# Eight of 36 split gate/up pieces: stored in pass one, or split again late in pass two; the third piece in the buffer of the sums

## The chip, the cores and the metric

The kernel runs on one core of a Trainium2 chip. The metric is the device time of one execution in microseconds (us), measured on the chip; lower is better. TensorE (PE in the profile), VectorE (DVE), ScalarE (ACT), GpSimd (POOL) and SyncE (SP, which here only issues transfers) run side by side, each through its own list of instructions in order. Transfers between HBM and the on-chip memory run on 16 DMA engines.

## The reference

x has 2048 rows of 576 numbers. It is normalized by rows (xn), and two branches take xn: an attention with 32 heads of 18 columns, and a bilinear gated unit with 4608 columns. The result is x + attention * silu(gated unit).

```python
qkv = xn @ wqkv                        # 32 heads of 18
p = softmax(q @ k.T * 18 ** -0.5)      # 2048 x 2048 for each head
s = concat(p @ v) @ wo
g = xn @ w_gate                        # 576 x 4608
u = xn @ w_up
b = (g * u) @ w_down                   # 4608 x 576
out = x + s * silu(b)
```

All is float32.

## The kernel before

**Numbers in two parts.** Products take float32r operands. Each operand is split into a rounded part (an ACT copy) and the rest (a POOL subtraction), and a product is three matmuls: high by high, rest by high, high by rest.

**Stages.** A prologue normalizes x, makes q, k and v and stores them to HBM. The main stage runs attention and the gated unit together in one list of PE instructions. The last stage multiplies by wo, forms silu of the last rows and writes out.

**The gated unit.** The 2048 rows are taken in NCH = 4 passes of 512 (c = 0 to 3). In each pass the 4608 columns are taken in NF2 = 18 units of 256, so there are 72 units; a unit u has two pieces, n = 2u and n = 2u + 1, 144 in all, and a piece is 128 columns of w_up and w_gate together. The columns go up in passes one and three and down in two and four (`columns_of`, L158), so the unit at a turn keeps its weights. PE's array is used as two halves of 64 rows with a stream of matmuls each (`stream`, L848): stream 0 multiplies the up columns of a piece, stream 1 its gate columns, 27 matmuls each (L678); `up_end` (L681) evicts on ACT (L683), `gate_end` (L685) multiplies on DVE (L690), then splits the product into hs on ACT (L693) and POOL (L694). The down product of unit u - 1 follows the two pieces of unit u in each stream (L720): it needs hs and hx, which is hs with the two halves of its rows exchanged by two transfers (`turn_round`, L700 to L710). Its results are added into `acc` by DVE (L746, L748).

**Gate and up weights.** In pass one, piece n is loaded raw (`g_raw`, L113: two transfers of 288 KB into one of the two `wraw` buffers), split by `g_get` (L169) as three "chores" of an ACT copy (L193) and a POOL subtraction (L194) each, and a fourth chore, `end` (L197), stores the split piece to HBM (`swg`, 1152 KB, L199) and loads the raw piece n + 2. In passes two to four `g_get` loads the split piece from `swg` (L185). Split pieces live in two `wgu` buffers; `gate_end` of piece n calls `g_get(n + 2)` (L691), since piece n's buffer is free then. The down weights have a like scheme with one buffer (`d_get`, L208; `draw`, `swd`, `wd`); `draw` is later used by silu of finished rows (`silu_store`, L781).

**Attention.** For each of 32 heads there are 64 "a" matmuls (L596), whose 128 x 512 results DVE reduces to row maxima (L598); then `max_rows` (L606) puts the maxima into the operands; then 64 "b" matmuls (L628), on which ACT takes the exponential (L630); then groups of up to seven key tiles are multiplied by v (L639), over the whole array.

**The order.** `order` (L1111) writes PE's list. It keeps a clock for each stream and guesses of when engines and transfers are done, and picks what comes next. Attention items have due times on this clock (`a_goal`, L929; `b_goal`, L932); the gated unit fills in. A stream may not begin piece n before `loaded[n - 2]` (L1082), which is set when gate piece n - 2 ends (L1178), with a guess of a 1.18 MB transfer for every piece, in pass one too. `there["h", u]` (L1182, L1171) is the guessed arrival of hx. `small` (L1003) hands out one chore at a time, when ACT is thought to be free. Matmuls wait on the chip only where the real event is later than the place in the list.

All transfers named above are issued by SP in the order in which the program emits them; each issue waits there for what it depends on.

Of the kernel before, what the change touches and what calls it, by code (L numbers as in the profile page):

```python
# [40 lines left out]
def kernel(  # L41
# [70 lines left out]

    def g_raw(f):  # L113
        raw = wpool.tile([128, 9, 128], FT, name="wraw", bufs=2)
        for r, m in enumerate((w_up, w_gate)):
            nc.sync.dma_start(raw[64 * r:64 * r + 64], m[:, 128 * f:128 * f + 128].rearrange("(b p) c -> p b c", p=64))
        return raw
# [45 lines left out]
    gdone, ddone = set(), set()  # L163

    def g_load(n):
        if n < 2 * NF2:
            graw[n] = g_raw(n)

    def g_get(n):  # L169
# [9 lines left out]
        if n > 1 and n // 2 % NF2 == 0:  # L179
            gw[n] = gw[n - 2]  # L180
            gdone.add(n)
            return
        w = gw[n] = g_tile()
        if n >= 2 * NF2:
            nc.sync.dma_start(w.bitcast(FT), swg[f])  # L185
            gdone.add(n)
            return
# [9 lines left out]
        def end():  # L197
            gdone.add(n)
            nc.sync.dma_start(swg[f], w.bitcast(FT))  # L199
            g_load(n + 2)  # L200

# [376 lines left out]
    with ExitStack() as mid:  # L578
# [106 lines left out]
        def gate_end(n, ps):  # L685
# [4 lines left out]
            nc.vector.tensor_tensor(h32, ps, h32, op=OP.mult)  # L690
            g_get(n + 2)  # L691
            hj = hs[u][:, j]
            nc.scalar.activation(hj[:, 0, :], h32, AF.Copy)  # L693
            nc.gpsimd.tensor_tensor(hj[:, 1, :], h32, hj[:, 0, :].bitcast(FT), op=OP.subtract)  # L694
            if u == 0 and j or u == len(units) - 1:
                turn_round(u, j)
# [3 lines left out]
        def turn_round(u, j):  # L700
# [5 lines left out]
            else:  # L706
                hx[u] = gp.tile([128, 2, 2, 512], FR, name="hx", bufs=1)
                js = slice(0, 2)
            for r in range(2):
# [401 lines left out]
        def order():  # L1111
            nonlocal na, nb
            load_v(0)
            feeds = [stream(0), stream(1)]
            heads.extend(next(f) for f in feeds)
            wait = None
            while any(heads) or na < TOTAL or nb < TOTAL or due:
# [35 lines left out]
                elif op is not None:  # L1153
# [8 lines left out]
                    if end:  # L1162
# [11 lines left out]
                        else:  # L1174
                            gated[n] = done
                            fin = engine("ACT", done + 0.05, 0.535)
                            fin = engine("POOL", fin + 0.05, 1.29)
                            loaded[n] = moved(done - 0.4, 1.18) if (n // 2 + 1) % NF2 else 0.0  # L1178
                            if n // 2 == len(units) - 1:
                                there["h", n // 2] = moved(fin, 0.524)  # L1180
                            elif n == 1:
                                there["h", 0] = moved(fin, 1.05)  # L1182
                            for _ in range(2):
# [10 lines left out]

        heads, stuck, parts, loaded, stacks = [], [False], {}, {}, []
        order()


# [115 lines left out]
```

## Time and profile before

| what | us |
|---|---|
| median of three runs | 2569.61 |
| lowest and highest of them | 2569.59, 2571.27 |
| the profiled execution, its own time | 2571.43 |
| its span in the profile | 2569.4 |
| prologue (up to the first main matmul) | 0 to 195 |
| main stage | 195 to 2501 |
| last stage | 2501 to 2569 |

The span is the time between the first and the last recorded instruction. Busy times of an engine are sums over its instructions. A busy PE says that at least one matmul was under way, not that both halves of its array had one; how many matmuls ran in a stretch (the number behind x) tells that.

### The profile page before, as it was taken

The numbers are of one execution on the slowest core, as the hardware profiler recorded it, in microseconds if no ns is written. First come the engines' busy times: TensorE is split into PE (matmuls) and PEld (weight loads), VectorE is DVE, ScalarE is ACT, GpSimd is POOL, SyncE is SP. The second block draws the span as 40 slices with busy tenths as digits, with TensorE's granted clock in tenths as the row PEclk, the third lists the DMA queues.
The fourth block names the chain that finished last, engine by engine and source line by source line (L and its number), as shares of the span: only waits on it lengthen the run. The fifth ranks groups of instructions, "written<-read, shape, count | busy, mean of one in ns | idle before, by whom it ended". The sixth has DMA issues, their size and how long they took to land.

```text
span 2569.4 us, 59203 instructions
## 1 busy us (share of the span) xinstructions
PE 2547.8 (99%) x24360; PEld 2111.1 (82%) x24360; DVE 1933.2 (75%) x3377; ACT 1467.1 (57%) x2688; POOL 594.8 (23%) x663
## 2 busy tenths in 40 slices
PE   8999999999999999999999999999999999999999
PEld 7899888878878888877888888777888877888878
DVE  6208778777778898777778888777888887778437
ACT  5222666666756665555665665555665655556651
POOL 3214434434421111111111111111111111111125
PEclk9999999999999999999999999999999999999999
DMA  7799988888886666665686656665686666654567
GB/s 243 235 284 278 263 226 225 232 225 220 221 206 186 176 182 177 175 179 155 179 197 173 179 175 184 176 170 154 179 204 166 180 184 176 175 174 146 159 189 248
DMA packets 195898, 504.58 MB, mean 196 GB/s; under 512 B 58112, under 2 KB 116352, under 8 KB 156588
## 3 DMA queue, kind: packets, MB, share of 16 engines
q1 hardware_dynamic: 185676, 489.05, 68.6%
q0 software_dynamic: 9952, 11.74, 1.7%
q8 instruction: 192, 3.15, 0.6%
q14 instruction: 78, 0.64, 0.1%
HBM read 312.21 MB, written 107.61 MB: 163 GB/s over the span
## 4 chain that ended last, share of the span: by engine, by line
PE 95%; DMA 3%; DVE 1%; SPq 0%; ACT 0%; issue 0%; POOL 0%; ACTq 0%; DVEq 0%
PE pg L678 34%; PE pg L639 18%; PE pg L720 16%; PE pa L596 12%; PE pb L628 8%; PE pg L402 2%; PE pa L348 2%; PE pb L348 2%; PE pg L1244 1%; DMA hx<-hs 1%; PE pb L1244 1%; PE pa L1244 1%; DMA sqk<-hl 0%; DMA ring<-sqk 0%; DMA xc<-sx 0%; DMA o<-sot 0%
## 5 line engine op out<-in xcount | busy, mean ns | idle before, releaser
L598 DVE TENSOR_REDUCE mx<-pa 128x1 f32<-128x512 f32 x2048 | 1367.1, 686 | 223.6 <-PE pa L596 104.8
L630 ACT ACTIVATE pt<-pb 128x512 f32<-128x512 f32 x2048 | 1161.9, 598 | 534.8 <-PE pb L628 465.5
L678 PE MATMUL pg<-xc,wgu 64*128 64x512 f32 x7776 | 1366.1, 388 | 0.7 <-DMA xc<-sx 0.5
L678 PEld LDWEIGHTS pg<-xc,wgu 64*128 64x128 f32 x7776 | 1051.7, 184 | 41.6 <-DMA xc<-sx 1.2
L628 PE MATMUL pb<-pair,ring 64*128 64x512 f32 x1997 | 777.4, 395 | 1.5 <-DMA ring<-sqk 1.5
L596 PE MATMUL pa<-pair,ring 64*128 64x512 f32 x2006 | 776.9, 393 | 1.8 <-DVE mx L598 1.8
L720 PE MATMUL pg<-wd,hs 64*128 64x288 f32 x3408 | 523.4, 292 | 0.0
L720 PE MATMUL pg<-wd,hx 64*128 64x288 f32 x3408 | 515.2, 292 | 2.4 <-DMA hx<-hs 2.4
L694 POOL TENSOR_TENSOR hs<-us,hs 128x512 fp32r<-128x512 f32 x144 | 186.2, 1293 | 1320.3 <-ACT hs L693 1285.6
L720 PEld LDWEIGHTS pg<-wd,hs 64*128 64x128 f32 x3408 | 459.8, 185 | 4.0 <-DVE acc L748 0.2
L720 PEld LDWEIGHTS pg<-wd,hx 64*128 64x128 f32 x3408 | 453.4, 185 | 6.5 <-DMA hx<-hs 3.0
L639 PE MATMUL pg<-pt,vt 128*32 128x512 f32 x4096 | 454.8, 594 | 0.7 <-DVE acc L748 0.6
L596 PEld LDWEIGHTS pa<-pair,ring 64*128 64x128 f32 x2006 | 364.3, 184 | 69.8 <-issue 52.8
L628 PEld LDWEIGHTS pb<-pair,ring 64*128 64x128 f32 x1997 | 362.5, 184 | 8.7 <-issue 1.9
L639 PEld LDWEIGHTS pg<-pt,vt 128*32 128x32 f32 x4096 | 125.5, 110 | 284.0 <-issue 278.9
L748 DVE TENSOR_TENSOR acc<-acc,pg 128x288 f32<-128x288 f32 x544 | 233.0, 443 | 22.4 <-PE pg L720 21.4
L645 DVE TENSOR_TENSOR oc<-oc,pg 128x512 f32<-128x512 f32 x69 | 47.1, 683 | 220.4 <-PE pg L639 213.7
L693 ACT ACTIVATE hs<-us 128x512 fp32r<-128x512 f32 x144 | 91.0, 632 | 151.0 <-DVE us L690 149.7
L194 POOL TENSOR_TENSOR wgu<-wraw,wgu 128x384 fp32r<-128x384 f32 x108 | 108.6, 1017 | 97.1 <-ACT wgu L193 84.6
L643 ACT ACTIVATE oc<-pg 128x512 f32<-128x512 f32 x32 | 19.2, 598 | 185.0 <-PE pg L639 179.0
L690 DVE TENSOR_TENSOR us<-pg,us 128x512 f32<-128x512 f32 x144 | 98.2, 682 | 26.9 <-PE pg L678 15.7
L618 POOL DMA_DIRECT2D pair<-mt x128 | 77.8, 613 | 166.4 <-DVE mt L613 162.3
(141 smaller groups left out, 1359.0 us busy)
## 6 DMA issues: line engine op xcount, KB each, us to landing
wgu<-swg SPq DMA_DIRECT2D x102, 1152.0 KB
hx<-hs SPq DMA_DIRECT2D x142, 512.0 KB
wd<-swd SPq DMA_DIRECT2D x50, 1152.0 KB
swg<-wgu SPq DMA_DIRECT2D x36, 1152.0 KB
pair<-sqk SPq DMA_DIRECT2D x192, 144.0 KB
ring<-sqk SPq DMA_DIRECT2D x384, 72.0 KB
swd<-wd SPq DMA_DIRECT2D x18, 1152.0 KB
sqk<-hl SPq DMA_DIRECT2D x32, 512.0 KB
```

The source lines that it names most:

```text
L194: nc.gpsimd.tensor_tensor(w[:, 9 + b:12 + b, :], raw[:, b:b + 3, :], w[:, b:b + 3, :].bitcast(FT), op=OP.subtract)
L348: nc.tensor.matmul(p, wq[b, a], xcs[c][:, e, :], start=n == 0, stop=n == len(PAIRS) - 1)
L596: nc.tensor.matmul(p, q[rows, t * 128:(t + 1) * 128], k[rows, c * 512:(c + 1) * 512], start=True, stop=True)
L598: nc.vector.tensor_reduce(mx[h][:, t, c:c + 1], p, axis=AX.X, op=OP.max)
L628: nc.tensor.matmul(p, k[rows, t * 128:(t + 1) * 128], q[rows, c * 512:(c + 1) * 512], start=True, stop=True)
L630: nc.scalar.activation(pt[t, c], p, AF.Exp, scale=scale)
L639: nc.tensor.matmul(p[32 * c:32 * c + 32, :], vt[h // 2][:, t, 6 * (h % 2):6 * (h % 2) + 32], pt[t, c], start=t == ts[0], stop=t == ts[-1])
L678: nc.tensor.matmul(ps, gw[n][half[r], a, :], xg[i][half[r], e, :], start=k == 0, stop=k == len(TERMS) - 1)
L690: nc.vector.tensor_tensor(h32, ps, h32, op=OP.mult)
L694: nc.gpsimd.tensor_tensor(hj[:, 1, :], h32, hj[:, 0, :].bitcast(FT), op=OP.subtract)
L720: nc.tensor.matmul(ps[:, 0:HALF], (hx if k else hs)[u][half[r], j, a, s * 128:(s + 1) * 128], dw[u][half[r], k, j, e, :], start=n == 0, st ...
L748: nc.vector.tensor_tensor(a, a, ps[:, 0:HALF], op=OP.add)
```

## The change

The split pieces with f < 8 (columns 0 to 1023, pieces n = 0 to 7 of pass one) are not stored in pass one. In pass two these columns come last, as n = 64 to 71; there they are loaded raw into the `draw` buffer (one buffer), split again by chores and stored to `swg` then, for passes three and four. The raw load of n = 64 is issued with `g_get(62)`, each further one by the chore `end` of the piece ahead of it.

Piece n = 2 gets a buffer of its own, the one that later holds the sums (`acc`), and is asked for at the start of `order`. So `gate_end` of pieces 0 and 1 asks for pieces 3 and 4, that of piece 2 for none, and from 3 on it is n + 2 as before. The hx transfers of unit 0 are issued in halves, after each of its two pieces. The guesses in `order` follow.

```diff
-    def g_raw(f):
-        raw = wpool.tile([128, 9, 128], FT, name="wraw", bufs=2)
+    def g_raw(f, tag, bufs):
+        raw = wpool.tile([128, 9, 128], FT, name="wraw", tag=tag, bufs=bufs)
...
+    UNSAVED = 8
+
+    def g_after(n):
+        return {0: 3, 1: 4, 2: None}.get(n, n + 2)
+
     def g_load(n):
         if n < 2 * NF2:
-            graw[n] = g_raw(n)
+            graw[n] = g_raw(n, "wraw", 2)
+        elif 4 * NF2 - UNSAVED <= n < 4 * NF2:
+            graw[n] = g_raw(2 * columns_of(n // 2) + n % 2, "draw", 1)
...
-        w = gw[n] = g_tile()
-        if n >= 2 * NF2:
+        w = gw[n] = accp.tile([128, 18, 128], FR, name="wg2", tag="acc") if n == 2 else g_tile()
+        anew = 2 * NF2 <= n < 4 * NF2 and f < UNSAVED
+        if n == 4 * NF2 - UNSAVED - 2:
+            g_load(n + 2)
+        if n >= 2 * NF2 and not anew:
             nc.sync.dma_start(w.bitcast(FT), swg[f])
...
             gdone.add(n)
-            nc.sync.dma_start(swg[f], w.bitcast(FT))
-            g_load(n + 2)
+            if f >= UNSAVED or anew:
+                nc.sync.dma_start(swg[f], w.bitcast(FT))
+            g_load(n + 1 if anew else n + 2)
...
-            g_get(n + 2)
+            if g_after(n):
+                g_get(g_after(n))
...
-            if u == 0 and j or u == len(units) - 1:
+            if u in (0, len(units) - 1):
                 turn_round(u, j)
...
-                hx[u] = gp.tile([128, 2, 2, 512], FR, name="hx", bufs=1)
-                js = slice(0, 2)
+                if u or j == 0:
+                    hx[u] = gp.tile([128, 2, 2, 512], FR, name="hx", bufs=1)
+                js = slice(0, 2) if u else slice(j, j + 1)
...
             load_v(0)
+            g_get(2)
...
-                            loaded[n] = moved(done - 0.4, 1.18) if (n // 2 + 1) % NF2 else 0.0
+                            if n != 2:
+                                loaded[g_after(n) - 2] = moved(done - 0.4, 1.18) if (n // 2 + 1) % NF2 else 0.0
...
-                            elif n == 1:
-                                there["h", 0] = moved(fin, 1.05)
+                            elif n < 2:
+                                there["h", 0] = moved(fin, 0.524)
...
-        heads, stuck, parts, loaded, stacks = [], [False], {}, {}, []
+        heads, stuck, parts, loaded, stacks = [], [False], {}, {0: 0.0}, []
```

## Rows read from the trace of the kernel before

**Rows 1.** The page: busy time of the engines, and the DMA share in 40 slices.

```profile
PE 2547.8 (99%) x24360; PEld 2111.1 (82%) x24360; DVE 1933.2 (75%) x3377; ACT 1467.1 (57%) x2688; POOL 594.8 (23%) x663
DMA  7799988888886666665686656665686666654567
```

**Rows 2.** Windows: stretch, length, busy (x count) of PE, PEld, DVE, ACT, POOL, clock, DMA share, GB/s.

```profile
200.00:205.00 5.00, 5.00 (x47) 4.96 (x45) 4.34 (x7) 0.60 (x1) 0.00 (x0) 1.00 1.00 336
210.00:215.00 5.00, 5.00 (x32) 3.76 (x32) 4.60 (x8) 1.40 (x3) 1.36 (x2) 1.00 1.30 213
275.00:280.00 5.00, 3.56 (x42) 3.32 (x44) 2.60 (x5) 2.24 (x5) 1.30 (x1) 1.00 0.85 249
280.00:285.00 5.00, 5.00 (x70) 4.96 (x68) 4.89 (x11) 3.71 (x8) 3.06 (x3) 1.00 0.82 228
```

**Rows 3.** Timeline of ACT: evictions of up pieces 1 and 2 (start, duration).

```profile
208.80 0.60 ACT L683 ACTIVATE us<-pg 128x512 f32<-128x512 f32 x1 [1.18 <-PE pg L678]
218.72 0.60 ACT L683 ACTIVATE us<-pg 128x512 f32<-128x512 f32 x1 [3.20 <-PE pg L678]
```

**Rows 4.** Timeline of POOL: the split of piece 2.

```profile
207.72 2.96 POOL L194 TENSOR_TENSOR wgu<-wraw,wgu 128x384 fp32r<-128x384 f32 x3
```

**Rows 5.** Timeline of PE: a down matmul of unit 2; in brackets the idle time before.

```profile
276.24 0.40 PE L720 MATMUL pg<-wd,hx 64*128 64x288 f32 x1 [2.23 <-DMA hx<-hs]
```

**Rows 6.** Timeline of SP: transfers issued ahead of hx of unit 2 (start, issue time).

```profile
253.64 0.33 SPq L199 DMA_DIRECT2D swg<-wgu  x1
...
260.85 0.34 SPq L199 DMA_DIRECT2D swg<-wgu  x1
...
264.19 3.28 SPq L710 DMA_DIRECT2D hx<-hs  x2
```

**Rows 7.** Chain of waits: the same hx, start and length.

```profile
266.87 11.50 DMA hx<-hs
```

**Rows 8.** Windows of longer stretches (columns as in rows 2).

```profile
195.00:335.00 140.00, 136.80 (x1314) 121.18 (x1316) 110.78 (x188) 64.40 (x122) 63.18 (x60) 1.00 1.03 270
...
735.00:775.00 40.00, 37.98 (x387) 30.51 (x385) 29.66 (x56) 24.13 (x43) 8.00 (x9) 1.00 0.75 187
1200.00:1320.00 120.00, 120.00 (x1186) 97.98 (x1184) 94.13 (x166) 70.97 (x128) 18.05 (x23) 1.00 0.69 181
```

**Rows 9.** The page: the stores of split pieces (count, KB each).

```profile
swg<-wgu SPq DMA_DIRECT2D x36, 1152.0 KB
```

**Rows 10.** Timeline of DVE: ends of gate pieces, in pass one and late in pass two.

```profile
390.22 0.68 DVE L690 TENSOR_TENSOR us<-pg,us 128x512 f32<-128x512 f32 x1
...
1208.21 0.68 DVE L690 TENSOR_TENSOR us<-pg,us 128x512 f32<-128x512 f32 x1
1223.65 0.68 DVE L690 TENSOR_TENSOR us<-pg,us 128x512 f32<-128x512 f32 x1
```

**Rows 11.** Timeline of SP: the store of the piece asked for at 390.22.

```profile
401.92 0.34 SPq L199 DMA_DIRECT2D swg<-wgu  x1
```

**Rows 12.** Windows: a stretch in which the transfers of pass two run.

```profile
1207.00:1214.00 7.00, 7.00 (x65) 6.55 (x65) 6.34 (x10) 4.78 (x9) 1.29 (x1) 1.00 0.96 268
```

**Rows 13.** Groups of instructions: the split's ACT step (busy, mean ns, idle before).

```profile
L193 ACT ACTIVATE wgu<-wraw 128x384 fp32r<-128x384 f32 x108 | 54.1, 520 | 2.0 <-DMA wraw<-in_B_w_gate_dram 2.0
```

**Rows 14.** Timelines at the first head's maxima: DVE, POOL, and PE's wait after it.

```profile
247.64 0.78 DVE L610 TENSOR_SCALAR mm<-m 128x16 fp32r<-128x16 f32 x1
...
247.36 2.00 POOL L194 TENSOR_TENSOR wgu<-wraw,wgu 128x384 fp32r<-128x384 f32 x2
...
250.26 0.50 PE L596 MATMUL pa<-pair,ring 64*128 64x512 f32 x1 [0.77 <-DVE mx L598]
```

**Rows 15.** One line of the kernel: L610, all 32 (duration min/median/max in ns).

```profile
L610 DVE TENSOR_SCALAR mm<-m x32: 174/174/1187, 247.6 to 2405.9; 128x16 fp32r<-128x16 f32 x32
```

**Rows 16.** Chain of waits near the end of the main stage.

```profile
2481.92 3.57 PE pg L639 x32
...
2487.67 5.00 PE pg L720 x68
```

## The prediction

> **What bounds the kernel now.** The page comes first: PE is busy 99% of the span, so no other engine is the bound, and DMA is nearly full only in the slices from the second to the tenth [rows 1]. But a busy PE can have half its array empty, so the next view is the count of matmuls. At 200 to 205 us, while only piece and "a" matmuls run, 47 of them fit in 5 us, 5.00 / 47 = 0.106 us each; at 210 to 215 the same kinds reach only 32, with PE still "busy 5.00" [rows 2]. At 275 to 280, with down matmuls, 42 run where the next 5 us hold 70 [rows 2]. Then the wide stretches: from 195 to 335 PE idles 140.00 - 136.80 = 3.20 us and DMA is at a share of 1.03; late in pass two (1200 to 1320) PE idles nowhere and DMA is at 0.69 [rows 8]. I read from this that time can be won nearly only in the first 140 us of the main stage, by two things.
>
> The first is the hold of stream 0. Up piece 1 is evicted at 208.80, up piece 2 only 9.92 us later, at 218.72 [rows 3]. Piece 2 was split by POOL from 207.72 to 210.68 [rows 4], since its buffer was free only when gate piece 0 had ended; and the order holds the stream by its guess of a 1.18 MB transfer from that end. PE doesn't idle there, it runs one stream.
>
> The second is hx of unit 2. SP issues it at 264.19, behind two stores of split pieces (253.64, 260.85) [rows 6]; in the chain its transfer takes 11.50 us from 266.87 [rows 7], and PE stands for 2.23 us until the first part is there [rows 5].
>
> **The change, part by part.**
>
> *Piece 2 in its own buffer.* Its raw weights are loaded before the main stage starts. The three ACT copies and three POOL subtractions move from 207.7 to about 195, where ACT and POOL have nothing to do (0.60 and 0.00 us busy at 200 to 205 [rows 2]), so the move itself costs nothing; without that cover it would cost POOL's 2.96 us [rows 4]. Stream 0 goes on with up piece 2 at about 209. Pieces 3 and 4 are then asked for when gate pieces 0 and 1 end, one piece earlier than they are needed, which is the old lead again. The gain is the empty half: 47 - 32 = 15 matmuls at 0.106 us = **1.6 us** [rows 2]. Bounds: 0 if another guess (hx, the next piece) holds the stream instead, 2.1 us if the stream held were full otherwise: 27 matmuls at 2 x 0.106 are 5.7 us, the evictions lie 9.92 apart [rows 3], and half of the 4.2 us between is 2.1. The halved hx of unit 0 is two more issues on SP; hx is needed some 10 us after, so I take 0 for it.
>
> *Eight stores fewer in pass one.* Two stores of 1152 KB go from ahead of hx of unit 2 [rows 6, 9], 2.36 MB, at 270 GB/s [rows 8] 8.7 us of the transfer queue. Then hx, complete at 266.87 + 11.50 = 278.37 [rows 7], would be complete near 269.6, ahead of PE's need at 276.24 - 2.23 = 274.0 [rows 5]. PE's wait goes whole: **2.2 us**. What is late next: unit 0's and unit 1's hx have no wait on PE now, and have fewer stores ahead too; the stores begin again with piece 8, behind hx of unit 2. The lower end is 0 (hx held by something else than the queue), the upper end all that PE idles from 195 to 335, 3.20 us [rows 8].
>
> *Eight pieces anew in pass two.* Removed: eight loads of 1.18 MB; added: eight raw loads (two issues each) of half that and eight stores of 1.18 MB, so 8 x 0.59 = 4.7 MB more in some 125 us. DMA stands at 0.69 there [rows 8], and 4.7 MB at 268 GB/s [rows 12] is 18 us, 0.14 more: still room. SP gets 8 issues more, and the store waits on SP for POOL where the load waited for PE; behind it stand hx and the attention's loads, as in pass one, where from 335 on PE loses nothing that I see. ACT gets 24 x 0.520 = 12.5 us [rows 13] on 70.97 of 120 busy [rows 8], POOL 24 us (three in 2.96 [rows 4]) on 18.05: neither becomes the bound.
>
> The new wait is that of the ACT copy for its raw piece: one `draw` buffer, so the raw load of the next piece is issued only after the split of this one. In pass one the store that follows a split came 401.92 - 390.22 = 11.7 us after the gate end that asked for it [rows 10, 11]; store and raw load are 1.77 MB, at 268 GB/s [rows 12] 6.6 us. So raw is there 18.3 us after that gate end. The next gate end comes 1223.65 - 1208.21 = 15.44 us after the first [rows 10], and its chores start at once or some us later. So ACT stands 0 to 2.9 us for each of seven pieces, the exponentials queued behind it, and PE waits for these through the two pb banks. A second bank lets PE go on for about one spacing of the exponentials (2048 of them, 32 x 64, over some 2300 us of main stage: 1.1 us), so PE loses 0 to 1.8 us a piece, 0 to 12.6 us in all. I take **0.5 us lost**, near the lower end, since chores are handed out only when ACT is thought to be free and the 11.7 us held a visit to the v product.
>
> *A collision of POOL and DVE.* At 247.64 the DVE step L610 took 0.78 us while POOL split a piece [rows 14]; its median is 174 ns [rows 15]; PE then waited 0.77 us for DVE [rows 14]. In pass two POOL's splits cover 24 of 125 us, and a head's maxima end about once in 70 us, so two such ends meet them with 0.2 each: 2 x 0.2 x 0.77 = 0.3 us lost; bounds 0 and 1.5. In pass one the same 0.77 may go as well, as the pieces move; so I count the two as 0 together. [...]
>
> **Sum.** -1.6 - 2.2 + 0.5 = -3.3 us against the profiled execution's own 2571.43, so 2568.1 (span 2566.1). That execution is 1.82 us above the median; against the median, 2569.61, the forecast is **2566.3 us**, 0.13% less. I take 0.2%, 5.1 us, as what a measurement of this kernel can tell from no change.
>
> **The rivals.**
>
> *More than the sum.* More may run below the full rate than the two waits tell: 275 to 280 lacks 28 of 70 matmuls [rows 2], 2.0 us by 5.00 / 70 = 0.071 each. Of these 2.0 us 5.00 - 3.56 = 1.44 are PE's idle time, 0.6 are not. With DMA free all of it may go: the hold's 2.1, all idle time of the stretch, 3.2 [rows 8], and 0.6 on each side of the stop, 6.5 us, less 0.5: 2563.6 us. For it: DMA at 1.03 over 140 us [rows 8], so every transfer there is late by its queue. Against it: only one wait of PE names a transfer. Chance 0.27.
>
> *The gain is handed back.* Attention's due times stand on the order's own clock. If the gated unit comes ahead by the hold's 1.6 us, the same "b" items are left at the end with less to fill in; the last group of v ends at 2485.5, only the down products of 5.00 us and the last unit stand behind it [rows 16]. Or stream 0 is held by the next guess, and the 1.6 us stay. Then only hx's wait is won: 2569.61 - 2.2 + 0.5 = 2567.9 us. Chance 0.22.
>
> *Raw too late in pass two (slower).* The place is the ACT copy of pieces 65 to 71, the price up to 1.8 us each. It decides from 1.2 us a piece on: 7 x 1.2 = 8.4 eats the 3.8 us and 4.6 more; at the full price 2569.61 - 3.8 + 12.6 = 2578.4, at the point of turning 2574.2 us. For it: the single buffer and the 18.3 us against 15.4. Against it: DMA's share is 0.69 there [rows 8], so a raw load often meets an empty queue. Chance 0.08.
>
> *The change doesn't do what it says, or the order is reshuffled.* If piece 2's buffer is freed late by its former owner, ACT waits at 195 and the hold stays. And with another order the turn from pass one to two, where PE idles 40.00 - 37.98 = 2.0 us [rows 8], may lose more or less: 2566.3 plus or minus 2.0, or at worst with no gain left, 2571.6. Chance 0.08.
>
> **How the numbers follow.** The forecast (0.35) is the likeliest: 2566.3. "More" lies beyond 0.2%, the forecast and "handed back" within, "raw too late" above; the last rival within, but for a small rest on either side. So faster 0.28, same 0.62, slower 0.10. The range goes from 2562.0 (the rival "more" with the upper ends) to 2571.6 (no gain and 2.0 us lost); raw at its price is left out.
>
> **What would show it.** Right: 45 or more matmuls in each 5 us from 205 to 220; up piece 2 evicted some 7.5 us after piece 1; no wait of PE for hx before 335; a DMA share below 1 from 195 to 265. Wrong: ACT waiting for `draw` from 1200 to 1340 with PE idle beside it; PE's idle time of 195 to 335 still above 2 us; or the stretch won and the last group of v at the same time as before.

## The result, and the profile after

The changed kernel takes 2580.74 us (median of six runs, 2578.21 to 2583.46), the kernel before 2571.32 beside it: a ratio of 1.0037 with an interval of 1.0027 to 1.0046. It is 9.4 us slower. The forecast was 2566.3, its range ended at 2571.6. The profiled execution took 2580.36, its span is 2578.5.

The page of the changed kernel first (to be held against [rows 1]; the second line is the DMA share in 40 slices):

```profile
PE 2551.0 (99%) x24360; PEld 2112.7 (82%) x24360; DVE 1931.3 (75%) x3377; ACT 1470.1 (57%) x2712; POOL 617.6 (24%) x687
DMA  7797989889785657567886656655686666655467
```

PE is busy 99% again, so the page tells nothing of the 9.4 us; only ACT and POOL have 24 instructions more each, the new splits. The windows of the changed kernel tell more (columns as in [rows 2]; the long ones all begin at 195, where the main stage begins):

```profile
195.00:335.00 140.00, 137.40 (x1339) 120.99 (x1339) 110.07 (x190) 64.77 (x124) 63.04 (x60) 1.00 0.83 209
...
210.00:215.00 5.00, 5.00 (x48) 4.28 (x46) 4.55 (x8) 1.88 (x4) 2.33 (x3) 1.00 1.15 215
...
275.00:280.00 5.00, 5.00 (x73) 5.00 (x71) 5.00 (x12) 4.64 (x9) 3.31 (x3) 1.00 0.72 169
...
1200.00:1320.00 120.00, 116.13 (x1120) 93.83 (x1118) 87.82 (x153) 71.95 (x136) 36.04 (x41) 0.99 0.78 197
...
195.00:1240.00 1045.00, 1040.05 (x10334) 863.14 (x10334) 841.75 (x1460) 641.81 (x1196) 319.79 (x335) 1.00 0.76 199
195.00:1300.00 1105.00, 1096.17 (x10882) 907.87 (x10882) 883.55 (x1531) 677.09 (x1264) 337.72 (x354) 1.00 0.76 200
```

The last two of the kernel before:

```profile
195.00:1240.00 1045.00, 1038.72 (x10309) 861.53 (x10309) 841.37 (x1456) 639.34 (x1181) 307.06 (x322) 1.00 0.77 207
195.00:1300.00 1105.00, 1098.72 (x10914) 910.30 (x10914) 888.37 (x1541) 674.59 (x1245) 316.73 (x334) 1.00 0.76 206
```

The start came as forecast: 48 matmuls at 210 to 215 where 32 were, 73 at 275 to 280 where 42 were [rows 2]. The last two pairs give a measure that the rest of this text uses, the **lead**: matmuls done from 195 us to a moment, less those that the kernel before had done by then, at 0.107 us each (an estimate: 47 in 5 us are 0.106 [rows 2], 179 in the 20 us from 200 of the changed kernel 0.112; down products, 288 columns instead of 512, at 0.06, since 64 of them ran in the 4 us from 2488 of the kernel before). At 1240 the lead is 10334 - 10309 = 25 matmuls, 2.7 us; at 1300 it is 10882 - 10914 = -32, -3.4 us (down products are equal in number there). So 6.1 us went between 1240 and 1300. (The table below was counted a little differently and has +2.9 and -3.2 at these moments: a few tenths of a lead say nothing.) PE's timeline of the changed kernel shows the waits there (and one at 258):

```profile
257.94 0.46 PE L639 MATMUL pb<-pair,ring 64*128 64x512 f32 x1 [2.55 <-DMA pair<-mt]
...
1242.48 0.49 PE L639 MATMUL pb<-pair,ring 64*128 64x512 f32 x1 [1.49 <-ACT pt L641]
1244.42 0.39 PE L733 MATMUL pg<-wd,hs 64*128 64x288 f32 x1 [0.52 <-DMA wd<-swd]
1261.84 0.49 PE L639 MATMUL pb<-pair,ring 64*128 64x512 f32 x1 [1.86 <-ACT pt L641]
...
1339.40 0.72 PE L689 MATMUL pg<-xc,wgu 64*128 64x512 f32 x3 [0.89 <-DMA xc<-sx]
```

Twice between 1240 and 1300 it waits for an exponential (pt). ACT's timeline says why: a copy of a new split (L203) stands ahead of it in ACT's list, and waits for its raw piece (the first two lines are evictions of up pieces 1 and 2, against [rows 3]: 7.29 us apart instead of 9.92).

```profile
208.50 0.58 ACT L694 ACTIVATE us<-pg 128x512 f32<-128x512 f32 x1
...
215.79 0.60 ACT L694 ACTIVATE us<-pg 128x512 f32<-128x512 f32 x1 [1.13 <-POOL wgu L204]
...
1241.42 0.52 ACT L203 ACTIVATE wgu<-wraw 128x384 fp32r<-128x384 f32 x1 [2.42 <-DMA wraw<-in_B_w_gate_dram]
...
1260.78 0.52 ACT L203 ACTIVATE wgu<-wraw 128x384 fp32r<-128x384 f32 x1 [2.43 <-DMA ring<-sqk]
```

The second of these waits bears the name of another transfer (ring), but the copy doesn't read it: by the events of the trace, the last part of the raw piece asked for at 1249.74 landed at 1260.70, together with the first parts of ring. The experiment e1 below settles it.

SP's list of the changed kernel shows what stood ahead of the raw loads:

```profile
1232.68 0.34 SPq L210 DMA_DIRECT2D swg<-wgu  x1
1233.13 0.61 SPq L116 DMA_DIRECT2D wraw<-in_B_w_up_dram  x1
1233.79 1.41 SPq L116 DMA_DIRECT2D wraw<-in_B_w_gate_dram  x1
1235.26 1.02 SPq L231 DMA_DIRECT2D wd<-swd  x1
...
1246.69 0.34 SPq L210 DMA_DIRECT2D swg<-wgu  x1
1249.05 0.65 SPq L116 DMA_DIRECT2D wraw<-in_B_w_up_dram  x1
1249.74 0.67 SPq L116 DMA_DIRECT2D wraw<-in_B_w_gate_dram  x1
```

The store of 1152 KB goes first, when POOL has finished; raw and wd queue behind it. POOL itself had begun late, behind an issue of L629 that waited for DVE:

```profile
1227.24 2.43 POOL L629 DMA_DIRECT2D pair<-mt  x4 [4.22 <-DVE mt L624]
1229.69 2.97 POOL L204 TENSOR_TENSOR wgu<-wraw,wgu 128x384 fp32r<-128x384 f32 x3
```

In the chain of waits, two transfers that now set the pace are wd and, at the turn to pass three, x:

```profile
1235.26 9.12 DMA wd<-swd
...
1329.81 9.55 DMA xc<-sx
```

### The profile page after: what moved, and what is told of

Its sections match the earlier page's. It is cut to its first block, busy times and chain, and to the rows that moved or that the text cites. A ratio compares the mean times of both kernels' runs of the same rounds, so it can differ in the third digit from the quotient of the medians.

```text
span 2578.5 us, 59303 instructions
## 1 busy us (share of the span) xinstructions
PE 2551.0 (99%) x24360; PEld 2112.7 (82%) x24360; DVE 1931.3 (75%) x3377; ACT 1470.1 (57%) x2712; POOL 617.6 (24%) x687
## 4 chain that ended last, share of the span: by engine, by line
PE 93%; DMA 3%; DVE 2%; SPq 0%; ACT 0%; issue 0%; POOL 0%; ACTq 0%; DVEq 0%
PE pg L689 34%; PE pg L650 17%; PE pg L733 15%; PE pa L607 11%; PE pb L639 8%; PE pg L413 2%; PE pa L359 2%; PE pb L359 2%; PE pg L1259 1%; DMA xc<-sx 1%; DMA ring<-sqk 1%; PE pb L1259 1%; DMA o<-sot 0%; PE pa L1259 0%; DMA sqk<-hl 0%; DVE mx L609 0%
## 5 line engine op out<-in xcount | busy, mean ns | idle before, releaser
L204 POOL TENSOR_TENSOR wgu<-wraw,wgu 128x384 fp32r<-128x384 f32 x129 | 129.5, 1016 | 115.4 <-ACT wgu L203 106.5
L629 POOL DMA_DIRECT2D pair<-mt x128 | 77.6, 612 | 158.8 <-DVE mt L624 152.1
```

The costliest lines, as they stand in the source:

```text
L204: nc.gpsimd.tensor_tensor(w[:, 9 + b:12 + b, :], raw[:, b:b + 3, :], w[:, b:b + 3, :].bitcast(FT), op=OP.subtract)
```

## The experiments

All eighteen are edits of the changed kernel, but for one that edits the kernel before. "Median" is against the kernel before on the same chip (2571.3 to 2572.3), "end" is the end of the last down product in the profiled execution against 2501.15 before, where the main stage ends. Leads and ends come from one profiled execution of each kernel, medians from 5 to 11. Executions of one kernel lie 3 to 8 us apart, and the profiled one is not always a typical one (e6's took 2571.47 where its median is 2574.99, e8's 2576.46 where it is 2573.69): what is worth how much goes by the medians, where it was lost by the leads. "The planner" is `order`, which writes PE's list.

| kernel | lead at 300 | 1240 | 1300 | 1360 | 1740 | 2440 | end | median |
|---|---|---|---|---|---|---|---|---|
| the change | +2.8 | +2.9 | -3.2 | -4.9 | -7.1 | -7.2 | +8.3 | +9.4 |
| e1_raw_first | +1.4 | +3.1 | -0.5 | -4.0 | -5.9 | -6.2 | +6.6 | +5.3 |
| e6_store_at_next_gate | +2.8 | +4.5 | +4.3 | +3.4 | +1.4 | -0.4 | +1.1 | +3.3 |
| e7_split_no_store | +1.5 | +2.2 | -0.6 | -0.6 | -2.7 | -3.0 | +3.4 | +0.6 |
| e3_no_split_anew | +1.1 | +1.7 | +1.8 | +1.7 | -0.2 | -0.7 | +1.1 | -0.5 |
| e2_no_second_store | -7.3 | -4.6 | -6.9 | -6.6 | -8.9 | -9.4 | +10.5 | +11.6 |
| e4_all_saved | -9.3 | -7.5 | -7.4 | -7.1 | -9.2 | -9.3 | +10.6 | +9.9 |
| e8_four_pieces | -2.7 | +0.3 | +0.4 | -0.1 | -2.1 | -4.2 | +5.1 | +2.0 |
| e10_stores_only | +3.3 | +1.5 | +1.4 | +1.4 | +1.3 | +1.2 | -2.0 | -3.1 |
| e14_new_list_only | +3.2 | +1.7 | +1.7 | +1.6 | +1.5 | +0.9 | +0.3 | +0.7 |
| e5_no_third_buffer | +4.0 | +3.2 | -0.6 | -0.7 | -0.6 | -1.6 | +2.4 | +5.0 |
| e9_both | +3.4 | +3.5 | +3.4 | +3.2 | +3.3 | +2.6 | -1.7 | +5.7 |
| e11_both_four | -1.2 | -1.8 | -3.6 | -3.6 | -3.2 | -3.5 | +4.3 | +1.8 |
| e15_old_list_store_first | +3.3 | +2.1 | -6.5 | -7.1 | -6.8 | -7.4 | +7.1 | +7.8 |
| e13_old_list | +3.3 | +1.0 | -5.7 | -6.0 | -5.9 | -6.5 | +6.3 | +11.2 |
| e12_before_store_later | -8.8 | -8.9 | -8.8 | -8.6 | -8.8 | -8.5 | +9.0 | +10.5 |
| e16_paced_5 | +3.4 | -7.3 | -13.4 | -13.9 | -14.1 | -14.3 | +15.0 | +13.0 |
| e17_paced_8 | +3.3 | +1.7 | -7.0 | -6.9 | -6.8 | -7.4 | +7.3 | +9.0 |
| e18_paced_8_store_at_once | +3.4 | +2.2 | +1.1 | +1.0 | +1.2 | +0.9 | -1.4 | -1.4 |

**The late part: raw first (e1).**

```diff
+            g_load(n + 1) if anew else None
             if f >= UNSAVED or anew:
                 nc.sync.dma_start(swg[f], w.bitcast(FT))
-            g_load(n + 1 if anew else n + 2)
+            g_load(n + 2) if not anew else None
```

> Late in pass two the chore behind a split issues the next raw load first and the store of the split piece second; PE's and ACT's lists stay word for word those of the changed kernel. Theory A (the loss is ACT standing for a raw piece whose load queues behind the store, with one raw buffer): the raw piece comes 1.18 MB, some 4.4 us, sooner, so the waits of 2.42 us at 1241 and near 1261 go, PE's idle time from 1235 to 1275 falls from 3.87 to under 1 us, and the time falls from 2580.7 to about 2575. Theory B (the 24 ACT copies and POOL subtractions themselves push the exponentials back): nothing changes, 2580.7, idle still near 3.9. Theory C (the whole traffic of the stretch is too much, so the down weights, hx and the x blocks come late): the same bytes, so 2579 to 2582.

2576.56 us, a ratio of 1.0019 (1.0010 to 1.0028): 4.1 us of the 9.4 are back. Theory A holds in the main: PE's waits for ACT are gone, and none of ACT's waits from 1200 to 1345 is for a raw piece. But 1.8 us of idle time are left near 1243 where it expected under 1, and C has a part too: the waits of PE from 1225 to 1345 name transfers alone (columns: engine, name and line that waits, what it waited for; us in total, times, longest):

```profile
PE pg L689 <- DMA xc<-sx: 2.4, 3, 1.4
PE pg L733 <- DMA wd<-swd: 1.8, 1, 1.8
```

**Stored early and not again (e2), nothing split anew (e3), all as before but the third buffer (e4).**

```diff
e2: -            if f >= UNSAVED or anew:
    +            if not anew:
e3: +        anew = False
    -            nc.sync.dma_start(w.bitcast(FT), swg[f])
    +            nc.sync.dma_start(w.bitcast(FT), swg[f if f >= UNSAVED else f + UNSAVED])
e4: -    UNSAVED = 8
    +    UNSAVED = 0
```

> All 36 pieces are stored in pass one as before; late in pass two the eight pieces are still loaded raw and split, but not stored again. The order of PE's work is that of the changed kernel. Theory A: the raw piece has no store ahead of it, the waits of ACT go, and so does the loss of 6 us from 1240 to 1270; if the early stores cost the 2.2 us that I thought, some of the start's gain goes too: 2573 to 2576. Theory B: the loss stays: 2580 to 2583. Theory C: 9.4 MB less from 1175 to 1300, so the loss goes as by A, and the lost 1.6 us at the turn to pass three (1330 to 1345) goes as well: 2572 to 2575.

> The first eight pieces are not stored in pass one, and in passes two to four eight other stored pieces are loaded in their places (so the gated unit uses other weights for those columns); nothing is loaded raw or split after pass one. It is the early part of the change alone. All theories of pass two: the start's gain of some 2.8 us of matmul work stays and nothing is lost late in pass two: 2571.3 - 2.8 = 2568.5. The rival that the early gain is handed back near the end: 2571.

> All 36 pieces are stored in pass one and loaded from there in passes two to four, as before; only the third piece keeps its own buffer and the guesses of the order go with it. If the early stores are what made PE wait for hx of unit 2, that wait of 2.2 us or more is there again and only the hold of 1.6 us is won: 2569.7. If the third buffer alone makes the gain, 2568.5, like the kernel without the eight stores. Slower than 2571.3 would say that the new order itself costs.

2582.88 (1.0030 to 1.0055), 2570.83 (0.9988 to 1.0006) and 2581.14 (1.0025 to 1.0050). e2 and e4 missed what was expected, and for the same reason, so e2 can't tell the price of the late stores. The third buffer without the missing stores loses 9.3 us by 300 (e4): SP stands behind stores that wait for POOL, and raw and hx stand behind SP. In e4, from 200 to 300:

```profile
SPq L210 <- POOL wgu L204: 20.3, 6, 7.0
```

e3 keeps what the start wins until 1360 and ends where the kernel before does. The change less e3 is 9.9 us: all of the net loss belongs to the splits in pass two, with the list that the planner writes for them (the lists of the two part near 1190).

**Without the third buffer (e5), store put off (e6), split but never stored (e7), four pieces (e8).** e6 and e8 have raw first, too.

```diff
e5: -        w = gw[n] = accp.tile(...) if n == 2 else g_tile()
    +        w = gw[n] = g_tile()
    -        return {0: 3, 1: 4, 2: None}.get(n, n + 2)
    +        return n + 2
e6: in end()        +            if anew: owed.append((f, w))
    in gate_end()   +            while owed:
                    +                f, w = owed.pop()
                    +                nc.sync.dma_start(swg[f], w.bitcast(FT))
e7: -            if f >= UNSAVED or anew:
    +            if f >= UNSAVED:
e8: as e6, UNSAVED = 4
```

> The changed kernel with its early part taken back in one point: piece 2 again waits for the buffer of piece 0, as before; the eight stores are still left out in pass one and the pieces split anew in pass two. If the third buffer is worth its 1.6 us and the loss lies wholly in pass two: 2582.3 us (the changed kernel's 2580.7 plus 1.6), and 2.0 to 2.8 us less work done by 240 us than in the changed kernel. If what the early part wins is handed back by the later order whatever it is: 2580.7 within 1. If the third buffer itself moves pass two into a bad place (the raw loads then meet the wd load), 2576 or less.

> Raw load first, as in the experiment before, and the store of a piece split anew is put off to the next gate end (some 5 to 8 us later in SP's list), behind the loads of wd and hx that stood behind it. PE's, ACT's and POOL's lists stay as they were. If the 5.7 us that were left with the raw load first (2576.6 against 2570.8 without anything anew) are the store's traffic ahead of wd and of the x of pass three in the queue: 2571 to 2573, and PE's waits for wd at 1243 (1.8 us) and for xc at 1330 (2.4 us) go. If they are the traffic itself (raw and store must pass at some time) or the chores: 2576 to 2577, with the waits for xc as before.

> Nothing of the eight pieces is stored, in pass one or in pass two; they are loaded raw and split anew in pass two, and passes three and four load eight other pieces in their place, so the output is not the reference's. Early part and PE's list are those of the changed kernel. If the store is the whole price of the new late work: as without any new split, 2570.8, within 1. If raw loads, copies and subtractions cost something themselves: above, up to 2576; from the run that stored all in pass one and did not store again, which lost 2.5 us at 1225 to 1255, I expect 2573.

> Four pieces (columns 0 to 511) instead of eight, raw load first and the store put off as in the run beside it. Pieces 4 to 7 are stored in pass one again. If the start needs only the first stores gone (pieces 0 to 3 lie ahead of hx of unit 2 in SP's list): no loss at the start, half of the work late in pass two, and at the places at 1243 nothing is split anew any more: 2570 to 2572. If the stores of pieces 4 to 7 are the ones that stand ahead of the third buffer's raw loads: a loss of some us at 260 to 300 as where all were stored: 2575 to 2580.

2576.68 (1.0010 to 1.0028), 2574.99 (1.0003 to 1.0020), 2572.23 (0.9999 to 1.0017), 2573.69 (1.0000 to 1.0017). e6 has nearly the whole lead at 1300 (+4.3): with raw first and the store behind wd, only 0.2 us go between 1240 and 1300, in an execution that was its fastest. But from 1360 to 1740 it loses 2.0, and so does every kernel of the table that has the third buffer (1.9 to 2.3), while none without it loses more than 0.2. The missing late store (e7) leaves +0.6, so raw loads, copies and subtractions cost about 1 us against e3, within what these runs can tell. e8 lies between its two expectations: half the stores back cost the start (-2.7 at 300), half the late work costs little.

e5 comes nearest to the last of its expectations, 2576, but not for the reason given there: without the buffer the kernel is 4 us faster, since its lead at 300 is larger (+4.0) and it loses nothing from 1360 to 1740. The loss for raw stays (from +3.2 to -0.6 between 1240 and 1300).

**Both repairs without the buffer (e9), stores alone (e10), four pieces (e11), the kernel before with its stores put off (e12).**

```diff
e9:  e5 and e6 together
e10: e3 and e5 together
e11: e9, UNSAVED = 4
e12 (kernel before), in end():
-            nc.sync.dma_start(swg[f], w.bitcast(FT))
             g_load(n + 2)
+            owed.append((f, w))
```

> Both repairs of the late part and the early part without the third buffer: piece 2 waits for piece 0's buffer as before, the eight stores are left out, raw first, the store put off to the next gate end. The list of PE is that of before up to about 1200 us, and from there that of the run without the third buffer. If the third buffer's new list is what loses over 1500 to 1735 (2.1 to 2.5 us in each kernel that had it, nothing in the one without it) and the late places are mended by the two moves: the start's gain of 3.8 us, less 1 at the turn and 2.3 at the end as without the third buffer, so 2571.2, between 2569 and 2572.5. If the third buffer was not the cause: 2575, as with it.

> Nothing but the eight stores left out: no third buffer, nothing split anew; passes two to four load eight other pieces in the place of the eight, so the output is not the reference's. The list of PE is that of before from the first matmul to the last. If the missing stores are worth what the run without the third buffer won at the start (3.8 us at 350), and nothing hands it back while the list stays: 2568.0, between 2567 and 2569. If the last products of attention bound the end whatever came before (the gain handed back): 2570.5 to 2571.7.

> As the run with both repairs and no third buffer, with four pieces instead of eight. Before stored pieces 4 to 6 at 236.56, 253.64 and 260.85, ahead of hx of unit 2, so if these three are what delays hx, its wait of 2.2 us is back and the start's gain is 1.5 or less; half of the late work costs about half of 3.3. Then 2571 to 2572.5. If the first four stores (9.4 / 2 = 4.7 MB from 201 to 230) are what puts the whole queue behind: the gain of 3.8 stays and 2569 to 2570 come out.

> The kernel before, with no piece left unsaved and none split anew; only the order on SP in pass one changes: after a split the raw load goes first and the store is put off to the next gate end, behind hx where that is issued there. The list of PE is that of before. If hx and raw only stood behind stores in the queue: PE's 2.2 us for hx of unit 2 go, 2569 to 2570. If the queue is simply full until 265 (a share of 1.03), the store put off meets the next split's copies, which wait for the buffer: 2572 to 2576.

2577.24 (1.0012 to 1.0030), 2568.47 (0.9977 to 0.9995), 2573.34 (1.0003 to 1.0020), 2582.05 (1.0027 to 1.0052). e10 has the same PE list as the kernel before from the first matmul to the last, so its -3.1 us is the worth of the eight missing stores by themselves. Its windows, the first against [rows 8]:

```profile
195.00:335.00 140.00, 139.23 (x1342) 122.28 (x1341) 113.18 (x193) 66.30 (x126) 63.05 (x60) 1.00 0.82 205
...
752.00:754.00 2.00, 1.34 (x8) 1.29 (x10) 0.00 (x0) 0.60 (x1) 0.00 (x0) 0.74 0.70 260
754.00:756.00 2.00, 2.00 (x14) 0.61 (x14) 0.69 (x1) 0.60 (x1) 0.00 (x0) 0.50 0.19 78
756.00:758.00 2.00, 2.00 (x20) 0.48 (x16) 0.00 (x0) 0.00 (x0) 0.00 (x0) 0.91 0.03 8
```

PE idles 0.77 us up to 335 instead of 3.20. The rows at 752 are where e10 gives 1.8 us of its lead back: after a stop at the turn to pass two the granted clock is down (below).

e11 shows that the stores which delay hx of unit 2 are those of pieces 4 to 7: with these back, PE waits 2.3 us for hx again. e12 missed: a store put off holds the buffer that the next split needs (ACT's waits, 195 to 340):

```profile
ACT wgu L194 <- DMA swg<-wgu: 19.8, 4, 8.2
```

e9 missed as well. Its pass two is whole (+3.4 at 1300, no wait of PE from 1200 to 1360) and its main stage ends 1.7 us ahead of before, yet its median is 5.7 us slower; the profiled execution is 4.2 us longer in its span (2573.6 against 2569.4). All of that is lost behind 2180, in a list of PE that is new from about 1180 on, and most of it in the last stage.

**The list apart from the work (e13, e14, e15).** e13 is e9 with the splits handed out beside the planner, so its PE list is that of before; e14 has the new list (that of e5 and e9) and none of the work; e15 is e13 with the store ahead of the raw load.

```diff
e13: -        chores.extend([(piece, (b,)) for b in (0, 3, 6)] + [(end, ())])
     +        (aside if anew else chores).extend([(piece, (b,)) for b in (0, 3, 6)] + [(end, ())])
     in small():
     +            if aside and free["ACT"] <= now + 0.1:
     +                f, a = aside.pop(0)
     +                f(*a)
e14: e10, and where anew, chores named piece and end that do nothing
e15: e13, with the order of end() in the change
```

> The run with both repairs and no third buffer, but the eight new splits are handed out beside the planner: they go out where its guess has ACT free, and nothing of them is entered on its clock. So the list of PE is that of before from the first matmul to the last, with the same work for SP, ACT and POOL as in the run with both repairs (2577.2). If what that run lost after 2180 (1.1 us at 2195, 1.5 at 2450, some 4 in the last stage) is the new list that the planner writes once the splits are on its clock: 2568.5 to 2570, faster than both kernels. If the late splits cost it by what they do on the chip: 2574 to 2577.

> The reverse: eight stores left out, nothing split anew (passes two to four load eight other pieces in their place, so the output is not the reference's), but the planner is told of the eight splits, whose chores do nothing. The list of PE is that of the run with both repairs and of the one without the third buffer. If the list alone is the cause: 2575 to 2577, as the run with both repairs. If it is the work: 2568.5, as with only the stores left out.

> The old list as in the first run of this group, but the store goes out ahead of the raw load as in the change itself. If ACT's waits for the raw piece cost PE what they did at 1270 to 1300 with the new list (3.9 us): 2572.5 to 2574. If they fall on places where the old list has more in hand: within 1 us of the first run of this group.

2582.68 (1.0033 to 1.0058), 2572.19 (0.9995 to 1.0013), 2579.21 (1.0024 to 1.0051). The new list alone costs 2572.19 - 2568.47 = 3.7 us with the same work, just clear of the uncertainty of such a difference (3.3 us). Of it 2.3 us show in the main stage (ends of +0.3 and -2.0), in places that have nothing to do with weights (PE's waits of e14, 2180 to 2502):

```profile
PE pg L741 <- DVE us L709: 1.7, 1, 1.7
PE pg L741 <- DVE acc L769: 1.1, 1, 1.1
```

e9 has the same two waits, of the same length. But e14 comes out 5 us below e9, so the list does not explain all that e9 loses. And e13 was no cure: the planner no longer knew of the copies and put one where the raw piece wasn't there yet (ACT stood 3.6 us in e13, 6.7 in e15), and from 1240 to 1300 they lost 6.7 and 8.6 us. e15 fits neither of its two expectations. In e15 there:

```profile
1241.00:1244.00 3.00, 0.10 (x1) 0.00 (x0) 0.60 (x1) 0.00 (x0) 0.00 (x0) 1.00 1.17 264
1244.00:1248.00 4.00, 0.25 (x1) 0.25 (x1) 0.00 (x0) 1.72 (x4) 1.12 (x2) 0.55 0.68 138
1248.00:1252.00 4.00, 4.00 (x22) 0.95 (x26) 0.00 (x0) 1.18 (x3) 1.79 (x2) 0.60 0.42 159
```

**The moment of the copies (e16, e17, e18).** The old list; copies go out only 5 or 8 us after the gate end that asks for them; in e18 the store goes right behind the next raw load.

```diff
e16, e17: +            if aside and free["ACT"] <= now + 0.1 and now >= rested[0]:
          (rested[0] = moment of the gate end + 5.0 or + 8.0)
e18: as e17, and in end():
-            if anew: owed.append((f, w))
+            if f >= UNSAVED or anew: nc.sync.dma_start(swg[f], w.bitcast(FT))
```

> As the run with the old list (2582.7), but a piece's three copies may go out only from 5 us on after the gate end that frees its buffer, by the planner's clock, so that its raw load, issued when the piece ahead was split, has time to land. In the old-list run one copy stood 3.6 us for its raw piece at 1244 and 5.8 us of work were lost there, and nothing else up to 2480. If that one place was the loss: 2572 to 2575, with 1 us or more ahead of before from 1260 to 2440. If the copies only come late elsewhere (PE waiting for a split piece): 2578 or more. That it beats before would need the last stage not to lose again: 2569 to 2571.

> The same with 8 us in place of 5. If 5 us still leave a copy waiting for raw at one of the shorter distances between two pieces, this one is faster by up to 3 us; if 8 us bring the split too late for its first matmul, PE waits for the split pieces and it is slower by as much. Else the same, 2570 to 2575.

> The old list with copies from 8 us on, and the store goes out right behind the raw load of the next piece instead of at the next gate end. In the run with the store put off (2580.6) ACT stood 16.6 us in three waits for a buffer whose store was still under way, 8.7 in one. If these waits are the loss of that run over 1250 to 1300 (8.7 us of work): 2571 to 2573. If the raw loads' waits come in their place, or ACT is simply asked at a bad moment: 2577 or more.

2584.53 (1.0039 to 1.0064), 2580.57 (1.0027 to 1.0055) and 2570.93 (0.9984 to 1.0003). e16 came out as its worse alternative and e17 above its range: a later copy alone is no cure; e18 came out as expected. In e17 the copies stood for a store that was put off, in e18 only for raw, mostly once (ACT's waits from 1200 to 1400, e17 and then e18):

```profile
ACT wgu L208 <- DMA swg<-wgu: 16.6, 3, 8.7
```

```profile
ACT wgu L208 <- DMA wraw<-in_B_w_gate_dram: 6.1, 3, 4.7
```

e18 does all the work of the change but for the third buffer, and takes 2570.93 where the kernel before took 2572.34: 10 us less than the change, and no measurable gain over before. No kernel that does the whole work was measurably faster than before.

## Why the prediction was wrong

**What held.** *Piece 2 in its own buffer*: the hold went (evictions 7.29 us apart, 48 matmuls at 210 to 215), and the lead at 240 is 24 matmuls, 2.6 us, more than the 1.6 of the sum. *Eight stores fewer*: e10's lead grows from 0.5 at 240 to 3.3 at 300, 2.8 us where 2.2 were forecast, and e11 brings the wait for hx back with the stores of pieces 4 to 7. *The collision of POOL and DVE* didn't show: from 1200 to 1345 PE waits for no DVE step, and the two steps of the kind of [rows 14] there took 0.18 and 0.17 us (L621, at 1226.31 and 1301.05). The 2048 reductions of the changed kernel took 0.647 to 0.695 us each, 0.647 to 0.694 in the kernel before.

**What the start's steps left out.** The gain of the third buffer is given back within 20 us, as what comes next was not moved forward. PE stands at 257.94 for 2.55 us, until the maxima of the next head are there (pair<-mt). POOL issued them at 249.52, at 249.94 in the kernel before; only PE had come sooner. Counts up to 240 and 260, the changed kernel and then the one before, and POOL's issues in the same order:

```profile
195.00:240.00 45.00, 45.00 (x431) 41.51 (x431) 40.74 (x66) 12.04 (x24) 19.74 (x18) 1.00 0.74 172
195.00:260.00 65.00, 62.40 (x610) 57.62 (x609) 57.45 (x99) 19.81 (x38) 32.09 (x31) 1.00 0.73 175
...
195.00:240.00 45.00, 45.00 (x407) 41.38 (x407) 40.65 (x67) 11.72 (x23) 19.07 (x18) 1.00 1.07 286
195.00:260.00 65.00, 64.23 (x610) 59.96 (x610) 59.22 (x100) 18.73 (x36) 32.09 (x31) 1.00 1.06 278
...
249.52 2.62 POOL L629 DMA_DIRECT2D pair<-mt  x4 [2.42 <-PE pg L733]
...
249.94 2.63 POOL L618 DMA_DIRECT2D pair<-mt  x4 [0.58 <-DVE mt L613]
```

At 260 both have done 610 matmuls, 192 of them down products: the term of 1.6 us is worth nothing, and the lead of +2.8 at 300 is what the missing stores win, as in e10. Besides, the list that the planner writes with the third buffer loses 2 us from 1360 to 1740. Whether the buffer costs more than it wins isn't settled: without it the change is 4.1 us faster (e5), with nothing split anew 2.4 (e10 against e3, within the uncertainty), with both repairs 2.3 us slower (e9 against e6, within it too). The rival "handed back" had the outcome of this term, a gain that doesn't last, but looked for it at the end of the main stage.

**The step that failed** is "I take **0.5 us lost**, near the lower end" for ACT's waits for raw, the only price in the sum for the work late in pass two. That work cost 9.9 us (the change less e3), and 4.1 of them went when raw was loaded first (e1). The bounds (0 to 12.6) held the truth, the choice did not. By the prediction's own steps, with two gate ends from DVE's timeline of the changed kernel:

```profile
1220.29 0.68 DVE L701 TENSOR_TENSOR us<-pg,us 128x512 f32<-128x512 f32 x1
...
1236.68 0.68 DVE L701 TENSOR_TENSOR us<-pg,us 128x512 f32<-128x512 f32 x1
```

Gate end at 1220.29, store at 1232.68, 12.4 us later (11.7 forecast); the raw piece is there at 1241.42, 21.1 us after that gate end (18.3 forecast); the next gate end came after 16.4 (15.4 forecast). So the raw piece came 4.7 us after that gate end instead of 2.9, and ACT stood 2.42 us for it. Waits of this size came at two pieces of seven. The ground given for the lower end, that chores are handed out when ACT is thought to be free, was empty: ACT is free, and waits at the copy; the planner's guess is one of a transfer for each piece, and holds nothing of a raw load behind a store. Raw first takes 4.1 us off (e1); that is what the order of store and raw costs.

**The step beside it** was the SP queue: "from 335 on PE loses nothing that I see", and a DMA share of 0.69 as "still room". A share over 120 us said nothing of a single transfer here: behind store and raw, wd took 9.12 us and x at the turn 9.55, and PE waited for both. With the store put behind them, PE's waits from 1200 to 1360 fall to 0.7 us in the profiled execution (e6, 4.2 from 1225 to 1345 in e1), and the lead at 1360 goes from -4.0 to +3.4. The medians differ by 2.0 only (5.3 to 3.3), less than these runs can tell.

**The rival "raw too late"** had the right place and mechanism with a chance of 0.08, but not the way to its time: 2578.4 stood on waits of 1.8 us at seven pieces and on the whole gain of the start, while 2580.74 came from waits at two, the clock behind one of them (below), the waits for wd and x, and a start that kept less. Read as a ladder of medians against before: stores gone -3.1 (e10, without the third buffer); with it -0.5 (e3); splits as well +0.6 (e7); and the late stores put off +3.3 (e6), at once but behind raw +5.3 (e1), ahead of raw +9.4. The last step is larger than the runs' uncertainty (about 2.3 us for a ratio, 3.3 for a difference of two), as is the whole; the ones between are not.

**The order reshuffled** had 0.08 and 2.0 us either way. Measured it was 3.7 us for the list with the splits (e14 against e10) and about 2 for that of the buffer, so in a program with a planned list it is a term of the sum and no remainder. Its size is luck: with the third buffer, where the list with the splits is another one, e7 is only 1.1 us above e3, copies and raw loads included.

**Slips that decided nothing.** DMA is nearly full in the third to the twelfth slice of [rows 1], not the second to the tenth. The range's lower end, 2562.0, has no working; the upper ends that it names, 2.1 + 3.2 + 1.2, give 2563.1. Of the signs of being wrong two came: ACT waiting for raw with PE idle beside it, and 2.60 us of idle time from 195 to 335.

**Open.** e9 ends its main stage 1.7 us early and still has a median 5.7 us above. Its last stage lasts 74.2 us from the last down product on, 68.2 in the kernel before; in the other kernels it lasted 67 to 72, and 70 in e5 and e14, which have e9's list. There PE waits three times for DVE, 4.8 us (2500 to 2560), for the first of these steps 1.2 us in the kernel before:

```profile
PE pa L1266 <- DVE hi L849: 3.5, 2, 2.1
PE pa L1266 <- DVE ys L1275: 1.3, 1, 1.3
```

Why that stage is longer was not tried. Nor was a second buffer for the raw pieces, the plainest way to let their loads start sooner.

## What to carry to other kernels

A transfer moved to a stage with "room" must be placed, not averaged: look at what stands behind it in the same queue, and let the load that somebody waits for go ahead of the store that nobody does, but not so late that the store holds the buffer of the next piece. Where a planner writes the list of the bound engine, run the new work with the old list and the new list without the work before believing either; the new list alone cost 3.7 us here, more than the 3.3 that the change was to win. A gain at the start counts only if what comes next is moved forward, too.

## What the runs showed of the hardware

*A wait of PE can cost more than its length.* The granted clock fell behind some of them. In the changed kernel, behind the wait of 1.86 us at 1261.84:

```profile
1260.00:1262.00 2.00, 0.16 (x2) 0.17 (x4) 0.80 (x2) 1.23 (x3) 0.62 (x1) 1.00 0.62 156
1262.00:1264.00 2.00, 2.00 (x19) 1.85 (x21) 1.46 (x3) 2.00 (x5) 1.39 (x2) 0.83 0.40 111
1264.00:1266.00 2.00, 2.00 (x15) 1.91 (x14) 0.56 (x2) 1.21 (x3) 1.01 (x1) 0.50 0.00 0
1266.00:1268.00 2.00, 2.00 (x18) 2.00 (x16) 1.52 (x4) 1.11 (x2) 0.00 (x0) 0.82 1.22 438
```

With 1.00 again from 1268 to 1270, the stretch lost 2 x (0.17 + 0.50 + 0.18) = 1.70 us of full clock; a 64 x 512 matmul took 0.62 us from 1264 to 1266 and 0.39 from 1268 to 1270. In windows of 0.1 us the clock is 1.00 up to 1263.3, 0.50 from 1263.4 to 1266.7 and 1.00 from 1266.8, so the values between stand here in windows that hold an edge. The same sum at 752 in e10 is 2 x (0.26 + 0.50 + 0.09) = 1.70, and in e15 at 1244 it is 4 x (0.45 + 0.40) = 3.40, twice that. By these sums the waits cost their length and 1.7 or 3.4 us more: of the 6.1 us that the change lost from 1240 to 1300, 3.87 are PE's three waits and 1.70 is the clock. Not every wait draws it: at 257.94 the changed kernel's 2.55 us left the clock at 1.00, and e1's 2.92 at the same place took it to 0.84, 0.50 and 0.81 from 256 to 262. The length doesn't decide it: at this place the clock fell behind 2.33 us in e7 (0.50 from 258 to 260) and stayed at 1.00 behind 2.63 in e6; in e3 it was 0.71, 0.50 and 0.93 from 258 to 264. That is why kernels with the same work and list up to here have +2.8 (the change, e6) or +1.1 to +1.5 (e1, e3, e7) at 300: a difference of luck, not of the edit.
